# Cached grouped-query attention on one core: K in 16 KB rows, PV three batches behind QK, wo loads on another queue

## The chip, the cores and the metric

The kernel runs on one core of a Trainium2 chip. The metric is the device time of the whole program in microseconds (us), the median of several executions. One execution per kernel is also taken by the hardware profiler; its span runs from the first to the last instruction. Engines are named as the profile names them: PE (TensorE matmuls), PEld (its weight loads), DVE (VectorE), ACT (ScalarE), POOL (GpSimd), SP (SyncE, which here only issues transfers; SPq is its queue).

## The reference

The inputs are `x` (32 batches x 4 positions x 1024), a key and a value cache of 32 x 4 heads x 2048 tokens x 128 each, `wq` (1024 x 4096) and `wo` (4096 x 1024), all bfloat16. There are 32 query heads; eight of them share one cached head.

```python
q = (x @ wq).reshape(B, Sq, Hq, Dh).transpose(0, 2, 1, 3)
k = jnp.repeat(k_cache, rep, axis=1)
v = jnp.repeat(v_cache, rep, axis=1)
scores = jnp.einsum("bhqd,bhkd->bhqk", q, k) * (Dh ** -0.5)
p = _softmax(scores, axis=-1)
o = jnp.einsum("bhqk,bhkd->bhqd", p, v)
return o.transpose(0, 2, 1, 3).reshape(B, Sq, Hq * Dh) @ wo
```

The caches are 67.1 MB each, `wq` and `wo` 8.4 MB each, so 151 MB are read for a result of 0.26 MB.

## The kernel before

**Tiling.** One batch's K is 2 MB, and so is its V. A batch has 4 heads x 8 query heads x 4 positions = 128 score rows, which fill the 128 partitions, against 2048 tokens: the scores of one batch are four PSUM banks (`ps_s`). `wq` and `wo` come as four loads of 2 MB each.

**Loads.** SP issues all loads in one order, the list `stream`: four parts of `wq`, K of batches 0 to 2, and from then on V of batch b and K of batch b+3 in turn, and the four parts of `wo` at the end, the last of them cut into four. Each load goes into one of nine slots in turn (`NSLOT`), and waits until the load that had this slot nine places earlier has been used up (`freed`): K when its last transpose is done, V when its PV is done. A load of K or V takes 128 partitions x 4 heads x 4096 bytes: the source is contiguous over 4 KB (16 tokens of one head).

**One batch.** PE transposes the K of a batch in eight fills of eight 128x128 tiles (`kt_fill`, L240) into four PSUM banks used in a ring (`ps_a`, `ps_b`, `ps_c`, `ps_o`); DVE copies five of the fills to `KT_sb`, ACT three (L353, L355). QK (`qk`, L285) multiplies 16 times, four heads side by side in the PE array. DVE takes the maximum (L379), ACT the exponential with the row sum (L408), DVE the reciprocal and a diagonal matrix of it (L388, L389). Four fills (`tr_fill`, L256) multiply P by that matrix, which transposes and normalizes at once; DVE and ACT copy them to `PT_sb` (L353, L355). PV (`pv`, L267) is 64 small matmuls into `ps_o`, copied by DVE to `oT_sb` (L368).

**Order on PE.** It is written out: QK of batch i, PV of batch i-1, the K transposes of batch i+2 (`AHEAD`), the P transposes of batch i. After the last batch comes PV of batch 31, and then the output projection (`oproj`, L318): 64 matmuls that accumulate over all of `wo`, and cannot start before every batch's output is in `oT_sb`. DVE and ACT copy the result out, half each (L398, L418), and SP stores it (L166).

**Waits.** Every operation names the events that it needs; `Program.emit` turns them into semaphore waits on its engine. There is no other scheduler.

Of the kernel before, what the change touches and what calls it, by code (L numbers as in the profile page):

```python
# [54 lines left out]
def bass_standalone__gqa_block_cached__sampling_kernel(  # L55
# [17 lines left out]
    G = Hkv  # L73
    scale = float(Dh) ** -0.5
    NSLOT = 9
    SLOT = 8192
    NRING = 4
    KT_FILLS = 2 * G
    TR_FILLS = 4
    AHEAD = 2  # L80
    WQ_LOADS = 4
    WO_LOADS = 4
    HPL = Hq // WO_LOADS

# [5 lines left out]
    with ExitStack() as es:  # L90
        sb = lambda name, shape, dt: es.enter_context(nc.sbuf_tensor(name, shape, dt))
        slots = sb("slots", [128, NSLOT, SLOT], BF16)
        KT_sb = sb("KT_sb", [128, 2, G, Sk], BF16)
        QT_sb = sb("QT_sb", [128, B, Hq, Sq], BF16)
        oT_sb = sb("oT_sb", [128, Hq, NT], BF16)
        pp_sb = sb("pp_sb", [128, 2, Sk], BF16)
# [6 lines left out]
        P_sb = pp_sb[:, 0, :]  # L103
        PT_sb = pp_sb[:, 1, :].rearrange("p (t r) -> p t r", r=128)
        x_sb = pp_sb[:, 0, 0:D]
        xT_sb = pp_sb[:, 0, D:2 * D].rearrange("p (a b) -> p a b", b=128)
        out_sb = pp_sb[:, 1, 0:D]
# [9 lines left out]
        for n in ["x", "out"] + [f"slot{i}" for i in range(NSLOT)] + [f"wo{i}" for i in range(4)]:  # L117
            pr.sems[n] = es.enter_context(nc.semaphore(f"s_{n}"))
# [3 lines left out]
        for b in range(AHEAD + 1):  # L122
            stream.append(("k", b))
        for b in range(B):
            stream.append(("v", b))
            if b + AHEAD + 1 < B:
                stream.append(("k", b + AHEAD + 1))
# [13 lines left out]
        pr.load("sp", lambda e: e.dma_start(x_sb, x_flat[:, :]), "x", "x", 16)  # L141
        for n, l in enumerate(stream):
            kind, i = l
            waits = [freed(stream[n - NSLOT])] if n >= NSLOT else []
            s, v = f"slot{n % NSLOT}", 16 * (n // NSLOT + 1)
            if kind == "wq":
                fn = lambda e, l=l, i=i: e.dma_start(slot(l), wq_v[:, i, :])  # L147
            elif kind in "kv":
                src = (k_cache if kind == "k" else v_cache)[i].rearrange("g (p t) d -> p g (t d)", p=128)
                fn = lambda e, l=l, src=src: e.dma_start(slot(l).rearrange("p (g f) -> p g f", g=G), src)  # L150
            if kind != "wo":
                pr.load("sp", fn, l, s, v, waits)
                continue
            last = i == WO_LOADS - 1
            parts = 4 if last else 1
            per = HPL // parts
            for q in range(parts):
                fn = lambda e, l=l, i=i, q=q, per=per: e.dma_start(
                    slot(l)[:, q * per * D:(q + 1) * per * D].rearrange("p (h n) -> p h n", n=D),
                    wo_v[:, i * HPL + q * per:i * HPL + (q + 1) * per, :],  # L160
                )
                if last:
                    pr.load("sp", fn, ("wo", i, q), f"wo{q}", 16, waits)
                else:
                    pr.load("sp", fn, l, s, v, waits)
# [3 lines left out]

        jobs = [("kt", b, f) for b in range(AHEAD) for f in range(KT_FILLS)]  # L170
        for i in range(B):
            if i + AHEAD < B:
                jobs += [("kt", i + AHEAD, f) for f in range(KT_FILLS)]
            jobs += [("tr", i, f) for f in range(TR_FILLS)]
        job_index = {j: n for n, j in enumerate(jobs)}
# [6 lines left out]

        def ring_waits(job):
            n = job_index[job]
            if n < NRING:
                return [("q_evac", n)]
            w = [("evac",) + jobs[n - NRING]]
            if n % NRING == 3:
                b = job[1] - AHEAD - 1 if job[0] == "kt" else job[1] - 1
                if b >= 0:  # L190
                    w.append(("ot", b))
            return w


        pr.op("pool", lambda e: e.memset(ident[:], 0.0), [], "zero")
        pr.op("pool", lambda e: e.affine_select(
            out=ident[:], in_=ident[:], compare_op=ALU.not_equal, fill=1.0, base=0,
            pattern=[[-1, 128]], channel_multiplier=1), ["zero"], "ident")
# [33 lines left out]
        def kt_fill(b, f):  # L232
            job = ("kt", b, f)
            dst = ring_bf16[job_index[job] % NRING]
            g, half = f // 2, f % 2

            def fn(e):
                for q in range(8):
                    t = half * 8 + q
                    ins = e.transpose(  # L240
                        dst[:, q * 128:(q + 1) * 128],
                        slot(("k", b))[:, (g * NKT + t) * Dh:(g * NKT + t + 1) * Dh],
                        ident[:, :],
                    )
                return ins

            pr.op("pe", fn, [("k", b)] + ring_waits(job), job)

        def tr_fill(b, f):
            job = ("tr", b, f)  # L250
            dst = ring_f32[job_index[job] % NRING]

            def fn(e):
                for q in range(4):
                    t = f * 4 + q
                    ins = e.matmul(dst[:, q * 128:(q + 1) * 128], lhsT=P_sb[:, t * 128:(t + 1) * 128],  # L256
                                   rhs=diag[:, b % 2, :], start=True, stop=True)
                return ins

            pr.op("pe", fn, [("exp", b), ("diag", b)] + ring_waits(job), job)  # L260

        def pv(b):
            def fn(e):
                v = slot(("v", b))
                for g in range(G):
                    for t in range(NKT):
                        ins = e.matmul(  # L267
                            ps_o[:, 32 * g:32 * (g + 1)],
                            lhsT=v[:, (g * NKT + t) * Dh:(g * NKT + t + 1) * Dh],
                            rhs=PT_sb[:, t, 32 * g:32 * (g + 1)],  # L270
                            start=(t == 0),
                            stop=(t == NKT - 1),
                        )
                return ins

            w = [("v", b)] + [("evac", "tr", b, f) for f in range(TR_FILLS)]
            if b > 0:
                w.append(("ot", b - 1))
            pr.op("pe", fn, w, ("pv", b))

        def qk(i):
            def fn(e):
                for c in range(Sk // 512):
                    for g in range(G):
                        ins = e.matmul(  # L285
                            ps_s[32 * g:32 * (g + 1), c * 512:(c + 1) * 512],
                            lhsT=QT_sb[:, i, REP * g:REP * (g + 1), :],
                            rhs=KT_sb[:, i % 2, g, c * 512:(c + 1) * 512],
                            start=True,
                            stop=True,  # L290
                            tile_position=(0, 32 * g),
                        )
                return ins

            w = [("evac", "kt", i, f) for f in range(KT_FILLS)]
            w += [("q_evac", j) for j in range(NB)] if i == 0 else [("exp", i - 1)]
            pr.op("pe", fn, w, ("qk", i))
# [13 lines left out]
        pv(B - 1)  # L311

        def oproj(i, h0, n, name):
# [15 lines left out]
        for i in range(WO_LOADS):  # L329
            last = i == WO_LOADS - 1  # L330
            parts = 4 if last else 1
            for q in range(parts):
                n = HPL // parts
                pr.op("pe", oproj(i, i * HPL + q * n, n, None),
                      [("wo", i, q) if last else ("wo", i), ("ot", B - 1), ("exp", B - 1)],
                      "oproj" if last and q == parts - 1 else None)


        def evac(job):
            eng = consumer(job)  # L340
            kind, b, f = job
            n = job_index[job]
            if kind == "kt":
                g, half = f // 2, f % 2
                src = ring_bf16[n % NRING]
                dst = KT_sb[:, b % 2, g, half * 1024:(half + 1) * 1024]
                w = [job] + ([("qk", b - 2)] if b >= 2 else [])
            else:
                src = ring_f32[n % NRING]
                dst = PT_sb[:, 4 * f:4 * f + 4, :].rearrange("p a b -> p (a b)")  # L350
                w = [job] + ([("pv", b - 1)] if b > 0 else [])
# [26 lines left out]
        for i in range(B):  # L378
# [3 lines left out]
            if i >= 1:  # L382
                ot_evac(i - 1)
# [13 lines left out]
        ot_evac(B - 1)  # L397
# [5 lines left out]
        for b in range(AHEAD):  # L403
            for f in range(KT_FILLS):
                if consumer(("kt", b, f)) == "act":
                    evac(("kt", b, f))
        for i in range(B):
            pr.op("act", lambda e, i=i: e.activation(  # L408
                P_sb, ps_s[:, :], ACT.Exp, bias=negmx[:, i:i + 1], scale=scale, accum_out=ssum[:, i:i + 1]),
# [61 lines left out]
```

## Time and profile before

| | |
|---|---|
| median of three executions | 389.32 us (388.3 to 391.09) |
| profiled execution: its time, its span | 388.88 us, 386.9 us |
| PE, PEld, DVE, ACT busy | 77%, 64%, 63%, 51% of the span |
| DMA, mean busy share of 16 engines | 98.5% for the queue that carries the loads |
| read from HBM | 151.26 MB, 392 GB/s over the span |
| mean granted PE clock | 0.938 |

A row of the timeline gives its start and its duration in us, the engine, the line, the operation, what it writes and reads, how often, and in brackets how long the engine sat idle before it and what ended that. A row of the windows gives, for a stretch of the span, the busy time of each engine, the granted PE clock, the DMA engines' busy share and the rate. The page's row "GB/s" gives the rate in 40 equal slices of 9.67 us. In the rows of the waits stand the engine and line that waited, what it waited for, the total, the number and the longest.

### The profile page before, as it was taken

To read this page: it belongs to the slowest core of one execution; us is meant where nothing else is said; L and a number is where in the kernel's file an instruction comes from. 1 tells how busy PE (TensorE), PEld (TensorE's weight loads), DVE (VectorE), ACT (ScalarE), POOL (GpSimd) and SP (SyncE) were. 2 spreads that over 40 slices of the span, in tenths; PEclk is the share of its full clock that TensorE was granted. 3 is DMA by queue.
4 is the path that set the end of the run, shared out by engine and by line. 5 is a ranking of instruction groups with operands and counts; after the bars stand their busy time and mean duration, and the time that the engine had idled before them with its cause. 6 is when DMAs were issued, how large, how long until landed. Compare 5 with 4: busy or idle time off the path is not lost.

```text
span 386.9 us, 11667 instructions
## 1 busy us (share of the span) xinstructions
PE 296.0 (77%) x5448; PEld 246.8 (64%) x5448; DVE 242.4 (63%) x390; ACT 196.6 (51%) x230; POOL 0.7 (0%) x6
## 2 busy tenths in 40 slices
PE   2877787776977977878788869877777787886596
PEld 1777576665766766767667657666666677664542
DVE  0026787775777777758777757877777577774400
ACT  1024766652655565466564635666555564664300
POOL 0000000000000000000000000000000000000000
PEclk9999999998999899889898979999999898997689
DMA  8999999999999999999999999999999999999981
GB/s 327 430 412 410 407 404 407 408 408 409 406 406 409 407 409 410 406 409 407 407 409 409 405 410 410 405 409 408 407 407 407 408 409 407 409 408 359 372 327 56
DMA packets 38912, 152.26 MB, mean 393 GB/s; under 512 B 1232, under 2 KB 1232, under 8 KB 38352
## 3 DMA queue, kind: packets, MB, share of 16 engines
q1 hardware_dynamic: 38864, 151.52, 98.5%
q8 instruction: 42, 0.69, 0.7%
q14 instruction: 6, 0.05, 0.0%
HBM read 151.26 MB, written 0.26 MB: 392 GB/s over the span
## 4 chain that ended last, share of the span: by engine, by line
DMA 87%; PE 7%; ACT 2%; DVE 2%; SPq 1%; issue 0%
DMA slots<-in_k_cache_dram 87%; PE ps_s L318 4%; DVE mx L379 1%; ACT pp_sb L408 1%; PE ps_s L285 1%; ACT KT_sb L355 1%; PE ps_a L240 1%; PE ps_o L267 0%; SPq L147 0%; PE ps_o L256 0%; PE ps_a L256 0%; PE ps_b L240 0%; SPq L150 0%; PE ps_c L256 0%; PE ps_b L256 0%
## 5 line engine op out<-in xcount | busy, mean ns | idle before, releaser
L408 ACT ACTIVATE pp_sb<-ps_s,negmx 128x2048 bf16<-128x2048 f32 x32 | 62.9, 1967 | 93.1 <-DVE negmx L380 93.1
L379 DVE TENSOR_REDUCE mx<-ps_s 128x1 f32<-128x2048 f32 x32 | 73.3, 2292 | 35.3 <-PE ps_s L285 35.3
L240 PE MATMUL ps_a<-ident,slots 128*128 128x128 bf16 x512 | 43.8, 234 | 42.2 <-DMA slots<-in_k_cache_dram 41.3
L240 PEld LDWEIGHTS ps_a<-ident,slots 128*128 128x128 bf16 x512 | 33.7, 105 | 46.1 <-DMA slots<-in_k_cache_dram 44.9
L267 PEld LDWEIGHTS ps_o<-pp_sb,slots 128*128 128x128 bf16 x2048 | 53.5, 96 | 14.6 <-issue 13.7
L267 PE MATMUL ps_o<-pp_sb,slots 128*128 128x32 bf16 x2048 | 56.7, 177 | 0.8 <-ACT pp_sb L355 0.8
L355 ACT ACTIVATE KT_sb<-ps_a 128x1024 bf16<-128x1024 bf16 x32 | 32.6, 1020 | 45.6 <-PE ps_a L240 45.6
L240 PE MATMUL ps_o<-ident,slots 128*128 128x128 bf16 x512 | 42.7, 231 | 7.8 <-DVE KT_sb L353 7.8
L353 DVE COPY KT_sb<-ps_b 128x1024 bf16<-128x1024 bf16 x64 | 43.7, 683 | 5.2 <-PE ps_b L240 5.2
L353 DVE COPY KT_sb<-ps_a 128x1024 bf16<-128x1024 bf16 x32 | 22.1, 689 | 35.0 <-PE ps_a L240 35.0
L240 PE MATMUL ps_c<-ident,slots 128*128 128x128 bf16 x512 | 43.3, 233 | 0.7 <-issue 0.7
L240 PE MATMUL ps_b<-ident,slots 128*128 128x128 bf16 x512 | 43.5, 234 | 0.0
L240 PEld LDWEIGHTS ps_o<-ident,slots 128*128 128x128 bf16 x512 | 33.8, 105 | 11.4 <-DVE KT_sb L353 11.2
L240 PEld LDWEIGHTS ps_c<-ident,slots 128*128 128x128 bf16 x512 | 34.8, 105 | 1.5 <-issue 0.9
L240 PEld LDWEIGHTS ps_b<-ident,slots 128*128 128x128 bf16 x512 | 35.2, 106 | 0.4
L285 PE MATMUL ps_s<-KT_sb,QT_sb 128*32 128x512 bf16 x512 | 34.3, 389 | 0.0
L355 ACT ACTIVATE KT_sb<-ps_c 128x1024 bf16<-128x1024 bf16 x32 | 32.7, 1021 | 1.9 <-PE ps_c L240 1.9
L355 ACT ACTIVATE KT_sb<-ps_o 128x1024 bf16<-128x1024 bf16 x32 | 32.9, 1027 | 0.0
L353 DVE CAST pp_sb<-ps_a 128x512 bf16<-128x512 f32 x32 | 22.1, 692 | 12.8 <-PE ps_a L256 12.8
L256 PE MATMUL ps_o<-diag,pp_sb 128*128 128x128 bf16 x128 | 13.2, 227 | 14.7 <-ACT KT_sb L355 14.7
L353 DVE CAST pp_sb<-ps_c 128x512 bf16<-128x512 f32 x32 | 21.9, 685 | 1.9 <-PE ps_c L256 1.6
L353 DVE COPY KT_sb<-ps_c 128x1024 bf16<-128x1024 bf16 x32 | 21.9, 684 | 1.0 <-PE ps_c L240 1.0
(46 smaller groups left out, 244.7 us busy)
## 6 DMA issues: line engine op xcount, KB each, us to landing
slots<-in_k_cache_dram SPq DMA_DIRECT2D x32, 2048.0 KB, 25.0
slots<-in_v_cache_dram SPq DMA_DIRECT2D x32, 2048.0 KB, 24.2
slots<-in_wq_dram SPq DMA_DIRECT2D x4, 2048.0 KB, 14.9
slots<-in_wo_dram SPq DMA_DIRECT2D x3, 2048.0 KB, 25.6
slots<-in_wo_dram SPq DMA_DIRECT2D x4, 512.0 KB, 12.2
pp_sb<-in_x_dram SPq DMA_DIRECT2D x1, 256.0 KB, 2.7
out_dram<-pp_sb SPq DMA_DIRECT2D x1, 256.0 KB, 2.2
```

The costliest lines, as they stand in the source:

```text
L240: ins = e.transpose(dst[:, q * 128:(q + 1) * 128], slot(("k", b))[:, (g * NKT + t) * Dh:(g * NKT + t + 1) * Dh], ident[:, :],)
L256: ins = e.matmul(dst[:, q * 128:(q + 1) * 128], lhsT=P_sb[:, t * 128:(t + 1) * 128], rhs=diag[:, b % 2, :], start=True, stop=True)
L267: ins = e.matmul(ps_o[:, 32 * g:32 * (g + 1)], lhsT=v[:, (g * NKT + t) * Dh:(g * NKT + t + 1) * Dh], rhs=PT_sb[:, t, 32 * g:32 * (g + 1)], ...
L285: ins = e.matmul(ps_s[32 * g:32 * (g + 1), c * 512:(c + 1) * 512], lhsT=QT_sb[:, i, REP * g:REP * (g + 1), :], rhs=KT_sb[:, i % 2, g, c * ...
L318: ins = e.matmul(ps_s[:, c * 512:(c + 1) * 512], lhsT=oT_sb[:, h, :], rhs=w[:, h - i * HPL, c * 512:(c + 1) * 512], start=(h == 0), stop=( ...
L353: pr.op("dve", lambda e: e.tensor_copy(dst, src), w, ("evac",) + job)
L355: pr.op("act", lambda e: e.activation(dst, src, ACT.Copy), w, ("evac",) + job)
L379: pr.op("dve", lambda e, i=i: e.tensor_reduce(mx[:, i:i + 1], ps_s[:, :], AX.X, ALU.max), [("qk", i)], ("max", i))
L408: pr.op("act", lambda e, i=i: e.activation(P_sb, ps_s[:, :], ACT.Exp, bias=negmx[:, i:i + 1], scale=scale, accum_out=ssum[:, i:i + 1]), [( ...
```

## The change

Four things change together.

- **K by rows of 16 KB.** The source of a K load is now read with 32 partitions for each head, each with 64 successive tokens: one partition's part is contiguous over 16 KB. A fill transposes 8 of these 64 tokens for all four heads, so `KT_sb` is laid out by token, head and partition, and QK reads its moving operand in pieces of 32 elements. QK is emitted in four parts, each waiting for its two fills.
- **P in the order of V.** V is still read with 16 successive tokens a partition. The exponential writes P with a step of four elements, so that a P transpose finds its 128 tokens in V's order.
- **PV three batches behind.** `LAG` is 3: PV of batch i-3 follows QK of batch i, K is loaded five batches ahead of V (`LEAD`), and `PT_buf` holds four batches. `NSLOT` is 8 in place of 9. The bank of each fill is now taken in turn as PE's order is written (`take`), and PV takes the fourth bank by name.
- **wo on GpSimd.** All of `wo` is loaded in 16 parts of 0.5 MB with a semaphore each, issued by POOL. Each part waits for its slot and for V of batch 30 to have landed.

```diff
-    NSLOT = 9
+    NSLOT = 8
...
+    LAG = 3
+    LEAD = AHEAD + LAG
+    NPT = LAG + 1
...
-        KT_sb = sb("KT_sb", [128, 2, G, Sk], BF16)
+        KT_sb = sb("KT_sb", [128, 2, KTOK, G, KP], BF16)
...
+        P_buf = sb("P_sb", [128, Sk], BF16)
+        PT_buf = sb("PT_sb", [128, NPT, NKT, 128], BF16)
...
-                src = (k_cache if kind == "k" else v_cache)[i].rearrange("g (p t) d -> p g (t d)", p=128)
-                fn = lambda e, l=l, src=src: e.dma_start(slot(l).rearrange("p (g f) -> p g f", g=G), src)
...
+            elif kind == "k":
+                src = k_cache[i].rearrange("g (p t) d -> (g p) (t d)", p=KP)
+                pr.load("sp", fetch(slot(l), src), l, s, v, waits)
+            elif kind == "v":
+                src = v_cache[i].rearrange("g (p t) d -> p g (t d)", p=128)
+                pr.load("sp", fetch(slot(l).rearrange("p (g f) -> p g f", g=G), src), l, s, v, waits)
+            else:
+                for q in range(WO_PARTS):
+                    part = slot(l)[:, q * WO_PER * D:(q + 1) * WO_PER * D].rearrange("p (h n) -> p h n", n=D)
+                    h0 = i * HPL + q * WO_PER
+                    pr.load("pool", fetch(part, wo_v[:, h0:h0 + WO_PER, :]), ("wo", i, q), f"wo{i * WO_PARTS + q}", 16, waits + [("v", B - 2)])
...
-                            rhs=KT_sb[:, i % 2, g, c * 512:(c + 1) * 512],
+                            rhs=KT_sb[:, i % 2, c * NKT:(c + 1) * NKT, g, :],
...
-            if i >= 1:
-                pv(i - 1)
+            if i >= LAG:
+                pv(i - LAG)
...
+        s_in = ps_s[:, :].rearrange("p (a t k) -> p a t k", a=A, k=KP)
+        p_out = P_sb.rearrange("p (t k a) -> p a t k", k=KP, a=A)
         for i in range(B):
             pr.op("act", lambda e, i=i: e.activation(
-                P_sb, ps_s[:, :], ACT.Exp, bias=negmx[:, i:i + 1], scale=scale, accum_out=ssum[:, i:i + 1]),
+                p_out, s_in, ACT.Exp, bias=negmx[:, i:i + 1], scale=scale, accum_out=ssum[:, i:i + 1]),
```

What stands on the engines, in rows of: line, operation, what it writes and reads, shape, count, and what it waits for. First SP's queue from its start, before and then now (`s_pe` is PE's count, by which a slot comes free):

```order
L141 DMA pp_sb<-in_x_dram 128x1024
L147 DMA slots<-in_wq_dram 128x8192 x4
L150 DMA slots<-in_k_cache_dram 128x4x2048 x3
L150 DMA slots<-in_v_cache_dram 128x4x2048
L150 DMA slots<-in_k_cache_dram 128x4x2048
L150 DMA slots<-in_v_cache_dram 128x4x2048 [waits s_pe]
```

```order
L150 DMA P_sb<-in_x_dram 128x1024
L157 DMA slots<-in_wq_dram 128x8192 x4
L157 DMA slots<-in_k_cache_dram 128x8192 x4
L157 DMA slots<-in_k_cache_dram 128x8192 [waits s_pe]
L157 DMA slots<-in_v_cache_dram 128x4x2048 [waits s_pe]
L157 DMA slots<-in_k_cache_dram 128x8192 [waits s_pe]
```

A K load has the shape of a `wq` load now, and five of them stand ahead of the first V.

Then the `wo` loads, before at the end of SP's queue, now on POOL (`s_slot2` is the landing of V of batch 30):

```order
L158 DMA slots<-in_wo_dram 128x8x1024 [waits s_pe] x3
L158 DMA slots<-in_wo_dram 128x2x1024 [waits s_pe]
L158 DMA slots<-in_wo_dram 128x2x1024 x3
L166 DMA out_dram<-pp_sb 128x1024 [waits s_act,s_dve]
L90 UNCONDITIONAL_BRANCH [waits s_out]
```

```order
L152 AFFINE_SELECT ident<-ident 128x128
L157 DMA slots<-in_wo_dram 128x2x1024 [waits s_slot2,s_pe]
L157 DMA slots<-in_wo_dram 128x2x1024 x3
L157 DMA slots<-in_wo_dram 128x2x1024 [waits s_pe]
L157 DMA slots<-in_wo_dram 128x2x1024 x3
```

Seven issues have become sixteen, on an engine that had nothing to do since its start.

Last, the end of PE's work, before and then now: QK of the last batch (L285), PV (L267, now L269), the P transposes (L256) and the output projection (L318, now L320):

```order
L285 MATMUL ps_s<-KT_sb,QT_sb 32x512 x16
L267 MATMUL ps_o<-pp_sb,slots 128x32 x64
L256 MATMUL ps_a<-diag,pp_sb 128x128 x4
L256 MATMUL ps_b<-diag,pp_sb 128x128 x4
L256 MATMUL ps_c<-diag,pp_sb 128x128 x4
L256 MATMUL ps_o<-diag,pp_sb 128x128 x4
L267 MATMUL ps_o<-pp_sb,slots 128x32 x64
L318 MATMUL ps_s<-slots,oT_sb 128x512 x64
```

```order
L285 MATMUL ps_s<-KT_sb,QT_sb 32x512 x16
L269 MATMUL ps_o<-PT_sb,slots 128x32 x64
L256 MATMUL ps_a<-diag,P_sb 128x128 x4
L256 MATMUL ps_b<-diag,P_sb 128x128 x4
L256 MATMUL ps_c<-diag,P_sb 128x128 x4
L256 MATMUL ps_o<-diag,P_sb 128x128 x4
L269 MATMUL ps_o<-PT_sb,slots 128x32 x192
L320 MATMUL ps_s<-slots,oT_sb 128x512 x64
```

Three PVs, of batches 29, 30 and 31, stand now between the last P transposes and the projection.

More of the change, by code (lines that the diff above doesn't have):

```diff
@@ L156, in bass_standalone__gqa_block_cached__sampling_kernel @@
[L156 to L165, printed above, removed]
+                pr.load("sp", fetch(slot(l), wq_v[:, i, :]), l, s, v, waits)
+            elif kind == "k":
[9 more added lines that the diff above has]
+                    pr.load("pool", fetch(part, wo_v[:, h0:h0 + WO_PER, :]), ("wo", i, q), f"wo{i * WO_PARTS + q}", 16, waits + [("v", B - 2)])
@@ L177, in consumer, with take @@
+        bank_last = {n: ("q_evac", n) for n in range(NRING)}
+        turn = [0]
+        def take(job, evac_event, bank=None):
+            if bank is None:
+                bank = turn[0] % NRING
+                turn[0] += 1
+            bank_of[job] = bank
+            before = bank_last[bank]
+            bank_last[bank] = evac_event
+            return bank, [before]
         def consumer(job):
@@ L181, in consumer @@
             return "dve" if f in (0, 2) else "act"
[L183 to L198, printed above, removed]
         def pe_xT(e):
@@ L258, in fn @@
                 return ins
-            pr.op("pe", fn, [("exp", b), ("diag", b)] + ring_waits(job), job)
+            pr.op("pe", fn, [("exp", b), ("diag", b)] + waits, job)
         def pv(b):
+            _, waits = take(("pv", b), ("ot", b), 3)
             def fn(e):
@@ L292, in fn @@
                         )
[L293 to L297, printed above, removed]
+                    return ins
+                w = [("evac", "kt", i, f) for f in range(2 * c, 2 * c + 2)]
+                if c == 0:
+                    w += [("q_evac", j) for j in range(NB)] if i == 0 else [("exp", i - 1)]
+                pr.op("pe", fn, w, ("qk", i) if c == A - 1 else None)
         for b in range(AHEAD):
@@ L310, in bass_standalone__gqa_block_cached__sampling_kernel, with oproj @@
                 tr_fill(i, f)
-        pv(B - 1)
-        def oproj(i, h0, n, name):
+        for b in range(B - LAG, B):
+            pv(b)
+        def oproj(i, h0, n):
             def fn(e):
@@ L329, in bass_standalone__gqa_block_cached__sampling_kernel @@
         for i in range(WO_LOADS):
[L330 to L336, printed above, removed]
+            for q in range(WO_PARTS):
+                pr.op("pe", oproj(i, i * HPL + q * WO_PER, WO_PER),
+                      [("wo", i, q), ("ot", B - 1), ("exp", B - 1)],
+                      "oproj" if (i, q) == (WO_LOADS - 1, WO_PARTS - 1) else None)
         def evac(job):
@@ L396, in bass_standalone__gqa_block_cached__sampling_kernel @@
                     evac(("tr", i, f))
-        ot_evac(B - 1)
+        for b in range(B - LAG, B):
+            ot_evac(b)
         pr.op("dve", lambda e: e.tensor_copy(out_sb[:, 0:512], ps_s[:, 0:512]), ["oproj"], "out0")
```

85 lines of the change are left out of this document (40 added, 45 removed).

## The prediction

> **What bounds the kernel now.** I read the page first: the rates by slice, the queues, the chain.
>
> ```profile
> span 386.9 us, 11667 instructions
> ...
> GB/s 327 430 412 410 407 404 407 408 408 409 406 406 409 407 409 410 406 409 407 407 409 409 405 410 410 405 409 408 407 407 407 408 409 407 409 408 359 372 327 56
> ...
> q1 hardware_dynamic: 38864, 151.52, 98.5%
> ...
> DMA 87%; PE 7%; ACT 2%; DVE 2%; SPq 1%; issue 0%
> ```
>
> One queue keeps the 16 DMA engines busy for 98.5% of the span, and the chain that ended last is 87% transfers. The rate is flat at about 408 GB/s while K and V come in, but not everywhere: 430 in the second slice, where `wq` is read, and 359 and 372 near the end, where `wo` is. Those three sorts of load differ in the length of the contiguous piece that goes to a partition: 16 KB for `wq` (two rows of 4096 bf16), 4 KB for K and V, 2 KB for `wo`. So I looked next at when PE is released by the first loads, in the timeline of the start.
>
> ```profile
> 19.91 0.45 PEld L215 LDWEIGHTS ps_a<-pp_sb,slots 128*128 128x128 bf16 x8 [2.55 <-DMA slots<-in_wq_dram]
> ...
> 24.82 0.45 PEld L215 LDWEIGHTS ps_a<-pp_sb,slots 128*128 128x128 bf16 x8 [1.33 <-DMA slots<-in_wq_dram]
> ...
> 29.92 0.45 PEld L240 LDWEIGHTS ps_a<-ident,slots 128*128 128x128 bf16 x8 [1.52 <-DMA slots<-in_k_cache_dram]
> ...
> 35.01 0.45 PEld L240 LDWEIGHTS ps_a<-ident,slots 128*128 128x128 bf16 x8 [1.45 <-DMA slots<-in_k_cache_dram]
> ...
> 40.14 0.45 PEld L240 LDWEIGHTS ps_a<-ident,slots 128*128 128x128 bf16 x8 [0.82 <-DMA slots<-in_k_cache_dram]
> ```
>
> All five starts are ended by a landing, and all five loads have 2.1 MB. The third to the fourth part of `wq` is 24.82 - 19.91 = 4.91 us; the three K loads behind it take (40.14 - 24.82) / 3 = 5.11 us each. The windows give the same two stretches as rates, and the long one behind them:
>
> ```profile
> 9.80:24.80 15.00, 11.49 (x184) 11.14 (x182) 0.00 (x0) 0.00 (x0) 0.00 (x0) 1.00 0.99 421
> 24.80:40.10 15.30, 12.36 (x208) 11.06 (x208) 9.17 (x15) 7.88 (x10) 0.00 (x0) 1.00 1.02 408
> 40.10:342.50 302.40, 238.30 (x4640) 202.53 (x4640) 217.80 (x350) 174.29 (x204) 0.00 (x0) 0.94 1.03 408
> ```
>
> Then the question whether compute keeps up. The waits say that PE is the one that waits, and the timeline of one batch shows by how much.
>
> ```profile
> PE ps_a L240 <- DMA slots<-in_k_cache_dram: 41.3, 30, 3.4
> ```
>
> ```profile
> 309.00 1.05 PE L285 MATMUL ps_s<-KT_sb,QT_sb 128*32 128x512 bf16 x16
> 309.97 1.77 PE L267 MATMUL ps_o<-pp_sb,slots 128*128 128x32 bf16 x64
> 311.89 0.62 PE L240 MATMUL ps_a<-ident,slots 128*128 128x128 bf16 x8 [0.15 <-DMA slots<-in_k_cache_dram]
> ...
> 317.87 1.05 PE L285 MATMUL ps_s<-KT_sb,QT_sb 128*32 128x512 bf16 x16
> ```
>
> With next to no wait a batch takes 317.87 - 309.00 = 8.87 us from QK to QK. The loads of a batch need 2 x 5.11 = 10.2 us. So compute has some 1.3 us a batch to spare, which is what PE waits (41.3 / 30 = 1.4). Last the end of the program:
>
> ```profile
> 342.52 0.45 PEld L240 LDWEIGHTS ps_a<-ident,slots 128*128 128x128 bf16 x8 [0.95 <-DMA slots<-in_k_cache_dram]
> ...
> 366.10 1.87 PE L267 MATMUL ps_o<-pp_sb,slots 128*128 128x32 bf16 x64 [0.78 <-ACT pp_sb L355]
> ...
> 368.45 14.86 PE L318 MATMUL ps_s<-slots,oT_sb 128*128 128x512 bf16 x64 [0.47 <-DVE oT_sb L368]
> ...
> 383.34 0.69 DVE L398 CAST pp_sb<-ps_s 128x512 bf16<-128x512 f32 x1 [15.04 <-PE ps_s L318]
> ```
>
> ```profile
> 378.00:380.00 2.00, 2.00 (x11) 0.94 (x10) 0.00 (x0) 0.00 (x0) 0.00 (x0) 1.00 0.16 61
> 380.00:380.50 0.50, 0.50 (x4) 0.20 (x3) 0.00 (x0) 0.00 (x0) 0.00 (x0) 1.00 0.00 0
> ```
>
> The last bytes of `wo` are in by about 380.0, but the projection runs 64 matmuls without a gap from 368.45 to 383.3 and never waits for them: its start is set by the last two batches, which take 25.9 us from the last K (342.52) to PV of batch 31 (368.4). From the last byte to the end of PE are 3.3 us, from there to the end of the span 3.6.
>
> **The change part by part.**
>
> *K rows.* 32 loads go from pieces of 4 KB to 16 KB. Transfers set the pace, so what a load saves comes off the span. Three readings: by landings 32 x (5.11 - 4.91) = 6.4 us; by the windows, 2.097 MB at 421 and at 408 GB/s are 4.98 and 5.14 us, 32 x 0.16 = 5.1 us; by the second slice at 430, 4.88 us, 32 x 0.26 = 8.3 us. I take the landings, since they are what compute waits for, and keep 5.1 and 8.3. [...]
>
> *Compute of a batch.* Fills, copies, PV and the 16 QK matmuls keep their number and shapes. Two access patterns are new. QK reads pieces of 32 elements: no row has that; between nothing and doubling its 1.05 us. The exponential writes every fourth element:
>
> ```profile
> L408 ACT ACTIVATE pp_sb<-ps_s,negmx 128x2048 bf16<-128x2048 f32 x32 | 62.9, 1967 | 93.1 <-DVE negmx L380 93.1
> L355 ACT ACTIVATE pp_sb<-ps_o 128x512 bf16<-128x512 f32 x32 | 19.1, 597 | 0.5 <-PE ps_o L256 0.5
> L363 ACT ACTIVATE QT_sb<-ps_s 128x512 bf16<-128x512 f32 x2 | 1.2, 597 | 0.6 <-PE ps_s L215 0.6
> ```
>
> L363 scatters its output in runs of four elements and takes 597 ns, the contiguous L355 of the same size as well. That is the nearest row, so I take nothing; the other end is a doubled exponential, +1.97 us a batch. In one batch the diagonal is ready while PE is still at the K fills:
>
> ```profile
> 219.77 0.25 DVE L389 TENSOR_SCALAR diag<-ident,rinv 128x128 bf16<-128x128 bf16 x1
> ...
> 221.13 0.39 PE L256 MATMUL ps_a<-diag,pp_sb 128*128 128x128 bf16 x4
> ```
>
> It is done at 220.0, and the P transposes start at 221.1. So 1.1 us of a longer exponential or QK are hidden there, and behind that the wait for K. That wait shrinks: loads of a batch will take 4.91 + 5.11 = 10.0 us, against 8.87.
>
> *LAG, LEAD, slots.* PV of batch i-3 no longer needs copies just made, but PV did not wait for them; it still waits for the fourth bank. Nothing gained in the stream. A pair (V of b, K of b+5) is used in one batch as the pair (V of b, K of b+3) was. Of eight slots one or two are in use and six on order, some 30 us of transfers; a load takes 25.0 and 24.2 us from issue to landing on the page, so most of that time is queue, and one slot less costs nothing as long as one load is outstanding. At the start five K's come ahead of V; batches 0 to 2 lack PV and compute falls behind by a few us, and catches up at over 1 us a batch. Nothing.
>
> *The end.* The last K now stands five V's ahead of the last V, 5 x 5.1 = 25.6 us earlier than it, where it stood three ahead. The two last batches and PV take 25.9 us from K, now with two PVs more at the end (2 x 1.9): PV of batch 31 ends some 4 us after its V has landed. Behind that V come 8.4 MB of `wo`, at 359 to 372 GB/s about 23 us, while the projection needs 14.9. So it no longer trails the transfers by its own length: its last part lands and four matmuls (4 x 14.86 / 64 = 0.9 us) remain, with a semaphore 1.1. Of 3.3 us 2.2 go.
>
> *wo on POOL.* Its issues start when V of batch 30 has landed, with V of batch 31 (5.1 us) still queued. For 16 issues there are 5.1 + 23 = 28 us, 1.75 each. No row shows an issue by POOL; the nearest are SP's own, with the queue empty and with it full:
>
> ```profile
> L147 SPq DMA_DIRECT2D slots<-in_wq_dram x4: 416/428/433, 1.2 to 2.6; - x4
> ...
> L158 SPq DMA_DIRECT2D slots<-in_wo_dram x7: 1295/3645/11213, 339.0 to 369.4; - x7
> ```
>
> Between 0.43 us and 1.3 all 16 are done in 7 to 21 us, inside the 28; I take nothing. POOL has nothing queued behind them, and SP's store no longer stands behind `wo`. V of batch 31 shares the engines with the first parts and lands later by up to 3 us; that leaves the sum of bytes as it is and the projection still ahead of `wo`.
>
> *Sum.* 386.9 - 6.4 - 2.2 = 378.3 us of span; the profiled execution lies 2.0 above its span and the median 0.4 above that: 380.7 us.
>
> **The rivals.**
>
> *K is not read faster (0.11).* `wq` is read at the start, with little else going on; K in 16 KB pieces alternates with V in 4 KB. [...] Against it: the step from 4.91 to 5.11 us falls exactly where the shape changes, with the engines as busy before as after. With nothing from K and the 2.2 of the end: 387.1 us.
>
> *POOL's issues set the pace of wo (0.13).* From 1.75 us each on, the sixteenth part comes after the engines have run dry. At 2.0 us the end moves by 16 x 0.25 plus a landing of about 2 us, 6 us: 387. [...] Against it: the 5.1 us in hand, and that seven issues became sixteen small ones of 256 pieces.
>
> *The exponential is slow with a step (0.08).* If it doubles, a batch goes from 8.87 us by 1.97 - 1.1 for what is hidden at the diagonal, and ACT's three K copies, which stand behind it, hold two of the ring's banks for the rest: up to 10.8 us a batch. It decides from 10.0 - 8.87 = 1.1 us on. Then compute sets the pace: 29 batches x (10.8 - 10.0) = 23 us, 404 us, slower. Against it: L363.
>
> **How the numbers follow.** The forecast gets 0.68. Its own range is 378.7 (8.3 from K) to 382 (5.1 from K); with up to a microsecond of luck below, and rivals one and two above, 377.5 to 387.5 leaves out the third rival and edges, under 0.2. Faster by over 1% is under 385.4: the forecast, some of the second rival (pace between 1.75 and 1.9) and part of the first (half a gain): 0.68 + 0.04 + 0.03 = 0.75. Within 1%: 0.17. Slower: 0.08. One per cent, 3.9 us, is about what a measurement of this kernel tells from no change; its three executions lie 2.8 apart.
>
> **What would show it.** Right: slices near 417 GB/s in the middle (the mean of 408 and 427, that is of 5.11 and 4.91 us), PE still waiting for K at L239, about 1 us a batch; the exponential at 1967 ns and QK at 1.05 us; the last `wo` part ending PE's last wait, and PE ending 1.1 us behind the last byte. Wrong: 408 in the middle (K), gaps in the transfers behind V of batch 31 with POOL at work (second rival), L408 over 3 us and no waits for K (third).

## The result: 469.97 us, a fifth slower

The changed kernel takes 469.97 us (469.51 to 471.34) against 389.06 us: a ratio of 1.208, 95% interval 1.202 to 1.213. Forecast were 380.7 us, in 377.5 to 387.5. The profiled execution's span is 469.4 us, 82.5 us more than before.

The page of the changed kernel, with the parts that answer to those shown of before; the last three rows are groups of instructions, with busy time and mean ns of one, and then the idle time before them and what ended it:

```profile
span 469.4 us, 11704 instructions
...
PE 332.0 (71%) x5446; PEld 258.7 (55%) x5448; DVE 242.1 (52%) x390; ACT 282.5 (60%) x230; POOL 12.3 (3%) x22
...
GB/s 329 430 427 427 412 414 416 422 422 359 309 350 328 351 328 305 356 311 329 317 355 327 307 353 334 338 348 311 358 306 316 328 342 318 279 333 348 7 1 24
...
q1 hardware_dynamic: 22368, 143.14, 78.8%
...
ACT 35%; PE 32%; DVE 24%; DMA 7%; issue 2%; SPq 1%
...
L408 ACT ACTIVATE P_sb<-ps_s,negmx 128x2048 bf16<-128x2048 f32 x32 | 154.0, 4812 | 112.6 <-DVE negmx L377 112.6
L239 PE MATMUL ps_o<-ident,slots 128*128 128x128 bf16 x512 | 47.7, 248 | 100.2 <-DVE KT_sb L350 100.2
...
L285 PE MATMUL ps_s<-KT_sb,QT_sb 128*32 128x512 bf16 x512 | 53.8, 564 | 0.0
```

Three things are to be seen. The exponential takes 4812 ns where it took 1967: that is 2.85 us a batch. The chain, which was 87% transfers, is now a chain of engines. And the transfers tell both stories: from the second slice to the ninth they run at 412 to 430 GB/s, as forecast, while the slots are filled; from the tenth on compute uses the loads more slowly than they come, and the rate falls to about 330.

One batch in the timeline, from QK to QK:

```profile
204.53 1.90 PE L285 MATMUL ps_s<-KT_sb,QT_sb 128*32 128x512 bf16 x16
...
206.48 2.29 DVE L376 TENSOR_REDUCE mx<-ps_s 128x1 f32<-128x2048 f32 x1 [1.59 <-PE ps_s L285]
...
208.99 4.82 ACT L408 ACTIVATE P_sb<-ps_s,negmx 128x2048 bf16<-128x2048 f32 x1 [3.76 <-DVE negmx L377]
...
214.04 0.25 DVE L386 TENSOR_SCALAR diag<-ident,rinv 128x128 bf16<-128x128 bf16 x1
214.21 0.68 DVE L350 COPY KT_sb<-ps_o 128x1024 bf16<-128x1024 bf16 x1
...
214.96 1.03 PE L239 MATMUL ps_o<-ident,slots 128*128 128x128 bf16 x8 [3.33 <-DVE KT_sb L350]
...
215.78 0.63 PE L256 MATMUL ps_a<-diag,P_sb 128*128 128x128 bf16 x4
...
217.65 1.90 PE L285 MATMUL ps_s<-KT_sb,QT_sb 128*32 128x512 bf16 x16
```

This batch is 13.1 us long; over all 32 it is 12.7 (QK of the first batch starts at 38.79, of the last at 432.82, 31 steps apart). DVE's queue holds the copy of the fourth K fill behind the reciprocal and the diagonal matrix, and these wait for the exponential. PE's last K fill needs the bank that this copy frees, so PE stands idle for 3.3 us. What it does after that is slow too: a fill of 1.03 us where 0.62 is usual, QK at 1.90 where it had 1.05. The windows of this batch show the granted clock of PE, the third number from the end: 1.00 before the wait, 0.50 behind it. Over the whole span the mean is 0.829, before it was 0.938.

```profile
208.00:211.60 3.60, 3.60 (x63) 3.14 (x59) 2.92 (x6) 2.61 (x1) 0.00 (x0) 1.00 0.90 344
211.60:214.95 3.35, 0.03 (x1) 0.00 (x0) 1.07 (x4) 3.35 (x4) 0.00 (x0) 0.84 1.02 405
214.95:216.50 1.55, 1.54 (x15) 1.55 (x16) 0.59 (x2) 1.09 (x2) 0.00 (x0) 0.50 0.29 116
```

### The profile page after: what moved, and what is told of

Same layout as the page of the kernel before. It is cut to its first block, busy times and chain, and to the rows that moved or that the text cites. A ratio compares the mean times of both kernels' runs of the same rounds, so it can differ in the third digit from the quotient of the medians.

```text
span 469.4 us, 11704 instructions
## 1 busy us (share of the span) xinstructions
PE 332.0 (71%) x5446; PEld 258.7 (55%) x5448; DVE 242.1 (52%) x390; ACT 282.5 (60%) x230; POOL 12.3 (3%) x22
## 4 chain that ended last, share of the span: by engine, by line
ACT 35%; PE 32%; DVE 24%; DMA 7%; issue 2%; SPq 1%
ACT P_sb L408 33%; DVE mx L376 16%; PE ps_s L285 11%; DMA slots<-in_k_cache_dram 7%; PE ps_o L239 6%; DVE KT_sb L350 4%; PE ps_o L256 3%; PE ps_s L320 3%; PE ps_c L256 2%; PE ps_b L256 2%; PE ps_a L256 2%; ACT KT_sb L352 2%; DVE diag L386 2%; DVE rinv L385 1%; PE ps_o L269 1%
## 5 line engine op out<-in xcount | busy, mean ns | idle before, releaser
L408 ACT ACTIVATE P_sb<-ps_s,negmx 128x2048 bf16<-128x2048 f32 x32 | 154.0, 4812 | 112.6 <-DVE negmx L377 112.6
L239 PE MATMUL ps_o<-ident,slots 128*128 128x128 bf16 x512 | 47.7, 248 | 100.2 <-DVE KT_sb L350 100.2
L269 PEld LDWEIGHTS ps_o<-PT_sb,slots 128*128 128x128 bf16 x2048 | 54.6, 99 | 23.1 <-issue 23.1
L269 PE MATMUL ps_o<-PT_sb,slots 128*128 128x32 bf16 x2048 | 57.7, 180 | 1.7 <-DVE oT_sb L365 1.0
L385 DVE RECIPROCAL rinv<-ssum 128x1 f32<-128x1 f32 x32 | 5.2, 164 | 96.8 <-ACT P_sb L408 96.8
L285 PE MATMUL ps_s<-KT_sb,QT_sb 128*32 128x512 bf16 x512 | 53.8, 564 | 0.0
L239 PE MATMUL ps_c<-ident,slots 128*128 128x128 bf16 x512 | 39.5, 220 | 0.0
L239 PE MATMUL ps_b<-ident,slots 128*128 128x128 bf16 x512 | 39.5, 220 | 0.0
L350 DVE CAST PT_sb<-ps_a 128x512 bf16<-128x512 f32 x32 | 22.1, 691 | 24.2 <-PE ps_a L256 24.2
L256 PE MATMUL ps_a<-diag,P_sb 128*128 128x128 bf16 x128 | 17.8, 284 | 12.5 <-DVE diag L386 12.5
L285 PEld LDWEIGHTS ps_s<-KT_sb,QT_sb 128*32 128x32 bf16 x512 | 13.5, 121 | 21.1 <-issue 19.7
L350 DVE CAST PT_sb<-ps_c 128x512 bf16<-128x512 f32 x32 | 22.1, 690 | 4.1 <-PE ps_c L256 3.9
```

The costliest lines, as they stand in the source:

```text
L239: ins = e.transpose(dst[:, q * 128:(q + 1) * 128], slot(("k", b))[:, t * Dh:(t + 1) * Dh], ident[:, :],)
L269: ins = e.matmul(ps_o[:, 32 * g:32 * (g + 1)], lhsT=v[:, (g * NKT + t) * Dh:(g * NKT + t + 1) * Dh], rhs=PT_buf[:, b % NPT, t, 32 * g:32 * ...
L285: ins = e.matmul(ps_s[32 * g:32 * (g + 1), c * 512:(c + 1) * 512], lhsT=QT_sb[:, i, REP * g:REP * (g + 1), :], rhs=KT_sb[:, i % 2, c * NKT ...
L350: pr.op("dve", lambda e: e.tensor_copy(dst, src), w, ("evac",) + job)
L385: pr.op("dve", lambda e, i=i: e.reciprocal(rinv[:, i:i + 1], ssum[:, i:i + 1]), [("exp", i)], ("rinv", i))
L408: pr.op("act", lambda e, i=i: e.activation(p_out, s_in, ACT.Exp, bias=negmx[:, i:i + 1], scale=scale, accum_out=ssum[:, i:i + 1]), [("negm ...
```

## The experiments

**Was it the exponential alone, and where else can the reordering go?** Three kernels keep everything else of the change and differ in the reordering of P: the first leaves it out, the other two have it at another place. A fourth puts eight forms of the exponential into the kernel before.

The first undoes the step:

```diff
-        s_in = ps_s[:, :].rearrange("p (a t k) -> p a t k", a=A, k=KP)
-        p_out = P_sb.rearrange("p (t k a) -> p a t k", k=KP, a=A)
+        s_in = ps_s[:, :]
+        p_out = P_sb
```

> The changed kernel with one thing undone: the exponential writes P contiguously, in the order in which it reads the scores. This leaves out the reordering of P to the order of V, so P and V do not match; every instruction keeps its count and size. Theory (the stepped write of the exponential alone turned the result): L408 back near 1967 ns, PE waits for K again, rates in the middle near 417 GB/s, and the time that was forecast, 379 to 382 us. Rival (QK in pieces of 32, the lag, eight slots or the issues by GpSimd cost as well): clearly more than 385 us, with PE or the transfers waiting at another place.

The second reads with the step and writes contiguously:

```diff
+        s_in = ps_s[:, :].rearrange("p (a u) -> p u a", a=A)
+        p_out = P_sb.rearrange("p (u a) -> p u a", a=A)
```

> The changed kernel with the reordering moved from the exponential's output to its input: P is written contiguously, the scores are read from PSUM with a step of 512 elements (2 KB). Theory (what costs is the stepped write of 2-byte elements to SBUF): L408 near 1967 ns, 379 to 382 us. Rival (any stepped access of ScalarE costs, or a read that hops between PSUM banks does): L408 at 4 us or more, 440 us or more.

The third has the exponential contiguous, and QK read K's columns in the order of V (so each of its four parts now waits for all eight fills of the batch, in place of two):

```diff
-                            rhs=KT_sb[:, i % 2, c * NKT:(c + 1) * NKT, g, :],
+                            rhs=KT_sb[:, i % 2, :, g, :].rearrange("p (a t) k -> p t k a", a=A)[:, 4 * c:4 * c + 4, :, :],
```

> The changed kernel with the reordering moved to PE: QK reads K's columns in V's order, with a step of 4 KB between neighbours, and the exponential is contiguous on both sides. If PE's moving read does not mind the step, QK stays at 1.05 us a batch and the time is 379 to 382 us. If every element costs as much as the stepped write did on ScalarE (2.4 times), QK takes 2.5 us, 1.5 more a batch than the 1.1 to spare, about 11.5 us x 0.4 on top: 385 to 395 us.

The fourth, on the kernel before:

```diff
+        forms = [
+            lambda i: lambda e: e.activation(P_sb, S, ACT.Exp, **kw(i)),
+            lambda i: lambda e: e.activation(step(P_sb, 2), S.rearrange("p (a u) -> p a u", a=2), ACT.Exp, **kw(i)),
+            lambda i: lambda e: e.activation(step(P_sb, 4), S.rearrange("p (a u) -> p a u", a=4), ACT.Exp, **kw(i)),
...
+            lambda i: lambda e: e.activation(step(P_sb, 4).rearrange("p a u -> p u a"), S.rearrange("p (a u) -> p u a", a=4), ACT.Exp, **kw(i)),
+        ]
...
-                P_sb, ps_s[:, :], ACT.Exp, bias=negmx[:, i:i + 1], scale=scale, accum_out=ssum[:, i:i + 1]),
+            pr.op("act", forms[i % 8](i),
```

> The kernel before with eight forms of the exponential in turn, batch by batch (so P's columns are in another order and the output is not the reference's): contiguous (L411); P written with a step of 2, 4 and 16 elements (L412, L413, L414); in pieces of two and of four elements with three such pieces between (L415, L416); contiguous with the scores read at a step of 4 (L417) and of 512 elements (L418). Theory (each write that touches a new piece of SBUF costs, so it is the bytes written next to each other that count): L411 1.97 us, L412 to L414 growing or level near 4.8, L415 about half of L413's excess, L416 at 1.97, L417 and L418 at 1.97. Rival (the shape of four rows of 512, not the step, costs): L412 to L416 all near 4.8, L417 too.

Measured, beside runs of the kernel before at 389.18 us (the first row: at 389.06 us):

| kernel | us | ratio to before, 95% interval | exponential, QK a batch |
|---|---|---|---|
| as changed | 469.97 | 1.208 (1.202 to 1.213) | 4.81 us, 1.05 to 1.9 us |
| contiguous (order of V left out) | 379.77 | 0.975 (0.973 to 0.978) | 1.97, 1.05 |
| PSUM read with a step | 379.45 | 0.975 (0.973 to 0.978) | 1.97, 1.05 |
| QK reads with a step | 429.91 | 1.105 (1.102 to 1.108) | 1.97, 3.6 |

The first theory holds for the whole: with the step undone the kernel lands 1 us under the forecast. The page of the kernel that reads PSUM with a step, which leaves nothing of the computation out, shows the forecast's marks: 413 to 420 GB/s in the middle, the exponential back, and PE waiting for K again.

```profile
span 377.5 us, 11704 instructions
...
GB/s 330 424 434 424 421 423 419 420 413 414 415 414 415 416 413 418 418 418 417 418 418 416 413 418 417 418 420 415 415 416 420 416 413 418 404 407 290 384 388 148
...
L408 ACT ACTIVATE P_sb<-ps_s,negmx 128x2048 bf16<-128x2048 f32 x32 | 62.9, 1967 | 93.1 <-DVE negmx L377 93.1
...
L239 PE MATMUL ps_a<-ident,slots 128*128 128x128 bf16 x512 | 41.2, 226 | 35.3 <-DMA slots<-in_k_cache_dram 31.4
```

So the same reordering costs 2.85 us a batch on the write side of ScalarE (4812 ns for 1967) and nothing on its read side (1967 ns), although there the step is 2 KB. On PE's read side it costs too, more than either expectation for that run: QK goes from 1.05 us to about 3.6, and every batch is 11.45 us long. The group of QK matmuls in that run:

```profile
L285 PE MATMUL ps_s<-KT_sb,QT_sb 128*32 128x512 bf16 x512 | 115.9, 1036 | 0.0
```

The eight forms, one line each, four executions each (the columns are the busy time of the group and the mean ns of one):

```profile
L414 ACT ACTIVATE pp_sb<-ps_s,negmx 128x2048 bf16<-128x2048 f32 x4 | 35.5, 8868 | 13.1 <-DVE negmx L380 13.1
...
L413 ACT ACTIVATE pp_sb<-ps_s,negmx 128x2048 bf16<-128x2048 f32 x4 | 19.3, 4821 | 11.6 <-DVE negmx L380 11.6
...
L412 ACT ACTIVATE pp_sb<-ps_s,negmx 128x2048 bf16<-128x2048 f32 x4 | 10.2, 2557 | 11.6 <-DVE negmx L380 11.6
...
L415 ACT ACTIVATE pp_sb<-ps_s,negmx 128x2048 bf16<-128x2048 f32 x4 | 8.4, 2112 | 14.3 <-DVE negmx L380 14.3
...
L411 ACT ACTIVATE pp_sb<-ps_s,negmx 128x2048 bf16<-128x2048 f32 x4 | 7.9, 1967 | 10.8 <-DVE negmx L380 10.8
L416 ACT ACTIVATE pp_sb<-ps_s,negmx 128x2048 bf16<-128x2048 f32 x4 | 7.9, 1967 | 11.6 <-DVE negmx L380 11.6
L417 ACT ACTIVATE pp_sb<-ps_s,negmx 128x2048 bf16<-128x2048 f32 x4 | 7.9, 1967 | 11.6 <-DVE negmx L380 11.6
L418 ACT ACTIVATE pp_sb<-ps_s,negmx 128x2048 bf16<-128x2048 f32 x4 | 7.9, 1967 | 12.5 <-DVE negmx L380 12.5
```

Contiguous (L411): 1967 ns. A step of 2, 4 and 16 elements (L412, L413, L414): 2557, 4821, 8868. Pieces of two elements (L415): 2112, and of four (L416): 1967, the same as contiguous, although they have the same four rows of 512 as L413. So the rival, that the shape costs, falls: it is the write of single 2-byte elements apart from each other. Reads with a step of 4 elements (L417) and with the step of the second kernel (L418) take 1967 ns too. The theory has the order right and not the sizes: the costs do not level off near 4.8 but still grow at a step of 16, and pieces of two elements, expected at half of L413's excess of 2.85 us, cost 0.15. That each write to a new piece of SBUF costs is not shown by these forms.

**What would a smaller excess have cost?** The kernel that reads PSUM with a step, but with a write at a step of 2 and a contiguous read:

```diff
-        s_in = ps_s[:, :].rearrange("p (a u) -> p u a", a=A)
-        p_out = P_sb.rearrange("p (u a) -> p u a", a=A)
+        s_in = ps_s[:, :].rearrange("p (a u) -> p a u", a=2)
+        p_out = P_sb.rearrange("p (u a) -> p a u", a=2)
```

> The kernel that reads the scores with a step, with the exponential reading contiguously and writing P with a step of 2 elements (the reordering of P to the order of V is left out). The eight forms gave 2557 ns for that write, 0.59 us more than a contiguous one. Theory (about 1.1 us of a longer exponential lie under the K fills and the rest of PE's wait for K covers what is left): 379 to 381, within 0.5 per cent of the contiguous one. Rival (the exponential is on the chain of every batch, nothing is hidden): 32 x 0.59 = 19 us more, 398 us.

Measured 379.82 us (ratio 0.977, 0.976 to 0.979), with the exponential at 2554 ns: the time is the theory's, 0.59 us a batch are hidden. But its 1.1 us under the K fills are not there; PE's wait for K does it all. That wait, which had been 31.4 us, shrinks to 19.4, and the wait for DVE's copy of the fourth fill, which had been 11.2, grows to 24.2. The rows of the waits, and one batch in which PE did not wait for K:

```profile
PE ps_o L239 <- DVE KT_sb L350: 24.2, 28, 1.3
PE ps_a L239 <- DMA slots<-in_k_cache_dram: 19.4, 14, 3.1
```

```profile
104.27 1.05 PE L285 MATMUL ps_s<-KT_sb,QT_sb 128*32 128x512 bf16 x16
...
111.63 0.62 PE L239 MATMUL ps_o<-ident,slots 128*128 128x128 bf16 x8 [1.11 <-DVE KT_sb L350]
...
113.70 1.05 PE L285 MATMUL ps_s<-KT_sb,QT_sb 128*32 128x512 bf16 x16
```

This batch takes 9.42 us, against 8.88 with the contiguous write: 0.54 of the 0.59 us come through. The time stays because 9.42 is still less than the 10.0 us that the loads of a batch need.

**Was it DVE's queue?** The changed kernel, with the copy of the fourth fill ahead of the reciprocal:

```diff
-            for job in fills[:3]:
+            for job in fills[:4]:
...
-            for job in fills[3:]:
+            for job in fills[4:]:
```

> The changed kernel itself, stepped write and all, with one copy moved on DVE: the fourth K fill is copied ahead of the reciprocal and the diagonal matrix, which wait for the exponential, instead of behind them. Theory (beside its own 2.85 us the long exponential holds DVE's queue, and with it the bank that PE's last K fill needs; PE then idles, and runs the next work at half clock): PE's wait at L239 for that copy, 100 us in all, goes, the batch of 13.1 us falls to 11.5 to 12.5, and the time by 20 to 45 us to 425 to 450. Rival (the chain from QK over the maximum, the exponential and the diagonal to the P transposes sets the batch by itself): 465 to 470, with PE waiting for the diagonal instead.

463.47 us, 6.5 less than as changed: the theory's size is wrong and the rival is nearly right. The wait for that copy is gone, but a wait of 73.9 us has come at the next place, where the first P transpose needs the bank of the fifth fill, whose copy stands behind the exponential on ACT:

```profile
PE ps_a L256 <- ACT KT_sb L352: 73.9, 30, 2.7
```

A batch is now 12.56 us long. So moving one copy exposes the next thing behind the exponential: in this kernel everything from the fifth fill on stands behind it, on one engine or the other.

**What the other parts of the change are worth.** Three kernels, all on the one that reads PSUM with a step (379.45 us). First with `wo` issued by SP again, in the same 16 parts:

```diff
-                    pr.load("pool", fetch(part, wo_v[:, h0:h0 + WO_PER, :]), ("wo", i, q), f"wo{i * WO_PARTS + q}", 16, waits + [("v", B - 2)])
+                    pr.load("sp", fetch(part, wo_v[:, h0:h0 + WO_PER, :]), ("wo", i, q), f"wo{i * WO_PARTS + q}", 16, waits)
```

> The kernel that reads the scores with a step (379.45 us) with one part undone: the 16 parts of wo are issued by SP again, behind the last V, each waiting for its slot alone. In the run with GpSimd the transfers fall from 416 to about 210 GB/s between 343 and 348 us, where the first wo part waits for V of batch 30. Theory (the engine that is last sets the end, and it is not the one that ran dry; the move of wo to GpSimd is worth nothing): 378.5 to 380.5. Rival (the dry stretch costs, 5 us at half the rate): 376.5 to 378. Second rival (GpSimd's transfers are the better ones): 381 or more.

Then this one with `LAG = 1` and `NSLOT = 9` in addition:

> The kernel that reads the scores with a step, with wo on SP and in addition PV one batch behind QK, K three batches ahead and nine slots, as in the kernel before: of the change only the 16 KB rows of K are left, with what they need in layout and 16 parts of wo. Theory by the terms of the sum: 6.4 us from K, nothing of the 2.2 us at the end, where the last two batches and the projection again follow the last K by their own length: 388.9 - 6.4 = 382 to 383. Rival (K's rows bring everything, lag and lead nothing): the same as the run beside it, within 0.8 us.

And with `wo` on GpSimd, but two V's earlier:

```diff
-                    pr.load("pool", fetch(part, wo_v[:, h0:h0 + WO_PER, :]), ("wo", i, q), f"wo{i * WO_PARTS + q}", 16, waits + [("v", B - 2)])
+                    pr.load("pool", fetch(part, wo_v[:, h0:h0 + WO_PER, :]), ("wo", i, q), f"wo{i * WO_PARTS + q}", 16, waits + [("v", B - 4)])
```

> The kernel that reads the scores with a step, with the wo parts on GpSimd, but waiting for V of batch 28 instead of batch 30 (and for their slots). The dry stretch at 343 to 348 us should be gone from the rates. Theory (the engine that is last sets the end): 379 to 380, unchanged. Rival (the dry stretch costs): 376.5 to 378.

| kernel | us | ratio to before, 95% interval |
|---|---|---|
| K rows alone (lag 1, nine slots, wo on SP) | 381.81 | 0.982 (0.980 to 0.983) |
| and lag 3, eight slots | 379.08 | 0.975 (0.973 to 0.976) |
| and wo on GpSimd, behind V of batch 30 | 379.45 | 0.975 (0.973 to 0.978) |
| wo on GpSimd, behind V of batch 28 | 384.65 | 0.989 (0.988 to 0.991) |

Before was 389.01 us beside the first, second and fourth, and 389.18 beside the third. So K's rows brought 7.2 us, together with QK in four parts and `wo` in 16, which that kernel keeps, and the lag 2.7 more. The intervals of the second and third kernel overlap: GpSimd brought nothing that these runs can tell. In the third the rate falls to 290 GB/s in the 37th slice, where POOL waits for V of batch 30, and it costs nothing either. In the kernel with lag 1 the projection starts late and never waits, as in the kernel before; with lag 3 it runs into its last parts and waits for each. The last QK, the last PV and the end of the projection's work, of the kernel with lag 1 and then with lag 3, both with `wo` on SP:

```profile
349.28 1.61 PE L285 MATMUL ps_s<-KT_sb,QT_sb 128*32 128x512 bf16 x16
...
358.80 1.87 PE L269 MATMUL ps_o<-PT_sb,slots 128*128 128x32 bf16 x64 [0.78 <-ACT PT_sb L352]
361.14 15.43 PE L320 MATMUL ps_s<-slots,oT_sb 128*128 128x512 bf16 x64 [0.48 <-DVE oT_sb L365]
376.61 0.69 DVE L396 CAST PT_sb<-ps_s 128x512 bf16<-128x512 f32 x1 [15.61 <-PE ps_s L320]
```

```profile
338.30 1.90 PE L285 MATMUL ps_s<-KT_sb,QT_sb 128*32 128x512 bf16 x16
...
357.20 9.40 PE L320 MATMUL ps_s<-slots,oT_sb 128*128 128x512 bf16 x40 [0.48 <-DVE oT_sb L365]
...
373.22 1.04 PE L320 MATMUL ps_s<-slots,oT_sb 128*128 128x512 bf16 x4 [0.24 <-DMA slots<-in_wo_dram]
374.30 0.69 DVE L396 CAST PT_sb<-ps_s 128x512 bf16<-128x512 f32 x1 [17.25 <-PE ps_s L320]
```

The earlier issue by GpSimd came out 5.2 us worse than the later one, against both expectations. The dry stretch is gone, but the `wo` parts share the engines with the last V's (from 325 to 382 us 38.4% of the engines' time goes to POOL's queue and 39.5% to SP's) and delay them, and the projection needs the last V before it needs any `wo`. PV of the last batch waits 4.8 us for V and the projection starts at 364.2 where it started at 357:

```profile
361.83 1.89 PE L269 MATMUL ps_o<-PT_sb,slots 128*128 128x32 bf16 x64 [4.78 <-DMA slots<-in_v_cache_dram]
364.19 15.09 PE L320 MATMUL ps_s<-slots,oT_sb 128*128 128x512 bf16 x64 [0.47 <-DVE oT_sb L365]
```

## Why the prediction was wrong

**The step that failed** is the price of the exponential: "L363 scatters its output in runs of four elements and takes 597 ns ... That is the nearest row, so I take nothing". That row holds for what it shows: in pieces of four elements the exponential takes 1967 ns, as contiguous (L416). The change writes single elements, for which no row stood in the profile, and that takes 4812 ns, 2.45 times as long. I took a row with a different contiguous length as the nearest one, and gave the case that no row covers 0.08.

**The bound failed too.** I capped it at a doubled exponential, +1.97 us; measured +2.85.

**The cover at the diagonal was not there.** "So 1.1 us of a longer exponential or QK are hidden there" takes the time from the end of the diagonal to the P transposes as slack. Between the two rows that the prediction shows stand these, in the kernel before:

```profile
219.94 0.68 DVE L353 COPY KT_sb<-ps_o 128x1024 bf16<-128x1024 bf16 x1
...
220.68 0.62 PE L240 MATMUL ps_o<-ident,slots 128*128 128x128 bf16 x8 [0.49 <-DVE KT_sb L353]
```

Before the change, too, DVE copies the fourth fill behind the diagonal, and PE's last K fill waits for that copy. So the 1.1 us are a chain of a copy and a fill. QK, the maximum, the exponential, the diagonal, this copy, the last fill and the P transposes follow each other, and this chain is the 8.87 us of a batch. Three runs bear that out, in batches in which PE does not wait for K: 0.59 us more of the exponential made a batch 0.54 longer, 2.57 more of QK made it 2.57 longer (11.45), and 2.85 more of the exponential would by that give 11.73. In the changed kernel the batches with a QK of 1.05 to 1.25 us (the first and the last aside, which lack other work) take 11.85 to 12.06 us, as this one (11.87):

```profile
77.26 1.06 PE L285 MATMUL ps_s<-KT_sb,QT_sb 128*32 128x512 bf16 x16
...
89.13 1.90 PE L285 MATMUL ps_s<-KT_sb,QT_sb 128*32 128x512 bf16 x16
```

The others take 12.7 to 13.1. What they have more is the work at a granted clock of 0.50 (0.50 to 0.52 in the windows of all their QKs): in the batch shown above QK is 0.85 us longer, and the last fill and the P transposes 0.63. The sum had no term for that. No run takes the wait alone away to see whether the clock stays up; in the kernel whose QK reads with a step PE waits 0.56 us in that place, not 3.3, and the mean granted clock is 0.984. So the mean of 12.7 us, where the third rival had "up to 10.8", is 8.87, the whole 2.85, and about 1 us of slower work. All that covers a longer exponential is the time by which the loads of a batch outlast 8.88 us, 10.0 - 8.88 = 1.1. The prediction had a second 1.1 us at the diagonal; only the upper end of the third rival, 8.87 + 1.97 = 10.8, went without it.

The rival's sign and its mark ("L408 over 3 us and no waits for K") were right: PE's waits for K fell from 41.3 to 2.2 us. Its mechanism was right in part: it named ACT's K copies, and what PE waited for was DVE's copy of the fourth fill, 100.2 us in all; ACT's came next, once that one was moved.

**K's rows: right.** Forecast 6.4 us, measured 7.2 in the kernel with K's rows alone. The landings that start PE stand 4.9 us apart for K as they had for `wq`, here in the timeline of the kernel that reads PSUM with a step:

```profile
29.45 0.45 PEld L239 LDWEIGHTS ps_a<-ident,slots 128*128 128x128 bf16 x8 [1.32 <-DMA slots<-in_k_cache_dram]
...
34.40 0.45 PEld L239 LDWEIGHTS ps_a<-ident,slots 128*128 128x128 bf16 x8 [1.30 <-DMA slots<-in_k_cache_dram]
...
39.30 0.45 PEld L239 LDWEIGHTS ps_a<-ident,slots 128*128 128x128 bf16 x8 [0.60 <-DMA slots<-in_k_cache_dram]
```

The rates in the middle are 413 to 420 GB/s against the forecast 417. The first rival, that K is not read faster, is excluded.

**The end: right.** Forecast 2.2 us, measured 2.7 (381.81 to 379.08). The last part of `wo` ends PE's last wait, as written. The 0.2 us for a semaphore was an estimate: in the chain of the kernel before PE starts 0.14 us behind DVE's last copy (368.31 to 368.45).

**wo on GpSimd: right in the sum.** POOL issued a part in 0.72 us, inside the 1.75 allowed, and the second rival did not come; its landing of about 2 us was an estimate, and the stores at the end, of 256 KB, took 2.0 to 2.2 us from issue to landing. What the prediction said of sharing ("lands later by up to 3 us; that leaves ... the projection still ahead of wo") holds for one V; with two more V's behind the first part, the fourth kernel shows the sharing deciding the end.

**QK in pieces of 32: right.** In the changed kernel it takes 1.05 us where the granted clock read 1.00 (the QKs at 38.8 and 268.5 us) and 1.90 where it read 0.50; in the kernel that reads PSUM with a step it takes 1.05 in every batch but the last, which takes 1.90.

**Cover by the transfers: right.** An excess of 0.59 us in the exponential cost no time. By the 1.1 us above, an estimate, an excess of more than that costs; no run lies between 0.59 and 2.57.

## What to carry to other kernels

When a layout change moves a permutation into an instruction, price that instruction by a row with the same contiguous length and the same side, read or write; without such a row, measure it, or give the case a chance that fits not knowing. The same permutation was free where ScalarE read it from PSUM (1967 ns, 379.45 us in all) and cost 20% where it was written (4812 ns, 469.97 us against 389.06). A gap between two rows is slack only if nothing between them hangs on the first: look for what the engine waited for there before counting it as cover. A stage that is hidden behind transfers by one microsecond (here 1.1) is not safe from an instruction that may more than double (here 1967 to 4812 ns).

## What the runs showed of the hardware

ScalarE's write to SBUF of 2048 bf16 elements takes 1967 ns contiguous or in pieces of 8 bytes (L411, L416), 2112 in pieces of 4 (L415), and for single elements 2557, 4821 and 8868 ns at steps of 4, 8 and 32 bytes (L412 to L414); its read of PSUM shows no such cost at a step of 2 KB (1967 ns, L418). Single elements 8 bytes apart (L413) and pieces of 4 bytes with 12 between them (L415) both go four times over the same 4 KB and write 512 elements each time, and take 4821 and 2112 ns. What sets the two forms apart is whether two elements are neighbours. Why it costs was not found. PE's moving read of single elements 4 KB apart made QK 3.4 times as long (3.6 us for 1.05). In the batch of the changed kernel that is shown above the granted clock of PE read 1.00 before a wait of 3.3 us and 0.50 in the 2.7 us behind it.
